# Two rings, a GpSimd-queue state load and a reordered first slot in the opening of an attention and MoE kernel

## The chip, the cores and the metric

The kernel runs on one core of one Trainium2 chip. The metric is device time of one execution in microseconds (us). "Median" is over all timed executions of a kernel in the state called fast; the profile is of one execution, and its span is some 2 us shorter than the time of that execution (205.1 us against 206.87 us for the kernel before). Engines are written as the profile has them: PE is TensorE, PEld its weight loads, DVE VectorE, ACT ScalarE, POOL GpSimd, SP SyncE.

## The reference, cut to what matters

```python
B, H, S, Ns, D = 8, 8, 512, 32, 64
def attn(x, state):                       # x [B,H,S,D], state [B,H,Ns,D]
    a = softmax(x @ state^T / 8)          # over the 32 state rows
    xread = a @ state
    a2 = softmax(state @ x^T / 8)         # over the 512 rows of x
    sread = a2 @ x
    return concat(xread, sread)           # [B,H,544,D] -> 4352 tokens of 512
def moe(x, w_in, w_out):                  # w_in [512,2048], w_out [2048,512]
    return gelu(x @ w_in) @ w_out
```

The kernel works batch by batch. The first Gelu of batch 0 can only start when x and state of batch 0 have been loaded, transposed, multiplied, exponentiated and normalised, and when a part of `w_in` is there. All that is "the opening", the first 12 of some 205 us.

## The kernel before

Cuts are marked with `# ...`. The inputs, all fp32, go either through a hardware ring (issued by SyncE or ScalarE; a cast follows on an engine) or through GpSimd's queue, whose target is a bf16 tile, with no cast behind it (in the list of DMA issues the state of batch 0 is 64.0 KB on ScalarE's ring, that of batch 1 32.0 KB on GpSimd's queue). All weights, and x of batches 1 to 7, are issued on GpSimd's queue, in program order.

```python
# opening, loads of batch 0: state and one quarter of x on ScalarE's ring, three quarters on SyncE's
nc.scalar.dma_start(out=st_f, in_=st_rows[:, 0, :, :])
for q in range(4):
    eng = nc.scalar if q == 2 else nc.sync
    eng.dma_start(out=x0f[:, q, :, :], in_=x0_rows[:, q, :, :])
# ...
nc.gpsimd.memset(sbd, 0.0)          # block-diagonal state, all eight batches
# ...
load_w_in(0, 256)                   # GpSimd's queue: the weight stream
load_w_in(256, 512)
load_w_out(0)                       # a quarter of w_out, 0.5 MiB in bf16
load_w_in(512, 1024)
load_st(1, 2)

def load_rest():                    # the stream after x of batch 1
    load_w_out(1); load_w_in(1024, 1536); load_w_out(2)
    load_w_in(1536, 2048); load_st(2, 3); load_x(2)
    load_w_out(3); load_x(3)

def keep_warm(n):                   # fillers: n x 128 columns of matmul on zeros
    ...

def state0():
    nc.scalar.copy(out=st_bf[:, 0, :, :], in_=st_f)    # cast
    # 5 transposes on TensorE, copies out of PSUM on VectorE
def cast0(q): ...                   # fp32 -> bf16 of one quarter of x
def xtr0(q): ...                    # its transposes and the copy out of PSUM
def scores0(q): ...                 # its scores and exp
def sums0(q): ...                   # its row sums
def norm0(t): ...                   # t = 0 multiplies on GpSimd, t = 1 on VectorE

keep_warm(31)
cast0(0); st0 = state0(); xtr0(0); cast0(1); state0_p(st0)
keep_warm(3)
cast0(2); xtr0(1); scores0(0); xtr0(2); cast0(3)
keep_warm(2)
scores0(1); sums0(0); xtr0(3); scores0(2)
keep_warm(2)
sums0(1)
load_x(1)                           # issue on GpSimd, ahead of the multiplication
norm0(0); scores0(3); sums0(2); sums0(3); norm0(1)
load_rest()
# ... P of batch 0 (attention folded with w_in) in two halves round the Gelu table load
# ... two matmul pairs "hp" and their Gelus, then the first slot
```

TensorE takes these instructions in program order.

The softmax here doesn't subtract the row's maximum and nothing guards it: scores larger than these inputs give would overflow.

## Time and profile before

| | before |
|---|---|
| time, median of 3 (later 4) runs | 206.78 us (206.87) |
| profiled span | 205.1 us |
| batch 0's state: landed, transposes start | 4.02, 4.61 us |
| first Gelu of batch 0 | 12.40 us |
| x of batch 2 landed | 31.53 us |
| scores of batch 2 start | 40.98 us |
| wait of TensorE for transposed x of batch 2 | 0.9 us |

From about 45 us on TensorE never stops (each stretch of 5 us up to 200 us reads 5.00 busy), so the end of the kernel is the moment at which the dense part starts plus a fixed amount of work. What sets that moment is the later of two arrivals near 41 us: TensorE itself, with the work of batches 0 and 1 behind it, and the transposed x of batch 2, which hangs on GpSimd's queue. In the trace of the kernel before, the x arrived last, by 0.9 us. The prediction shows the lines.

### The profile page before, as it was taken

How to read it: one execution, taken by the hardware profiler on the slowest of the kernel's cores; microseconds unless marked ns; L12 is line 12 of the kernel's file. 1: busy time of each engine (PE TensorE's matmuls, PEld its weight loads, DVE VectorE, ACT ScalarE, POOL GpSimd, SP SyncE). 2: the span in 40 equal slices, each digit the busy share in tenths (PEclk: the TensorE clock that was granted, in tenths of full speed). 3: DMA queues.
4: the chain of work that ended last, by engine and by line, in shares of the span. 5: the costliest groups of instructions: out<-in, count | busy, mean ns of one | idle time of the engine just before them, and what ended most of it. 6: DMA issues, size and time to landing. Idle time of an engine off the chain costs nothing.

```text
span 205.1 us, 4749 instructions
## 1 busy us (share of the span) xinstructions
PE 198.5 (97%) x1982; PEld 133.7 (65%) x1988; DVE 142.7 (70%) x227; ACT 134.3 (65%) x242; POOL 69.5 (34%) x74
## 2 busy tenths in 40 slices
PE   7899999899999999999999999999999999999994
PEld 2545444346776567766776777667775788778893
DVE  2944786989499868976697757765778553165883
ACT  3864786689696679675967697587857476744120
POOL 8964303632319645371626602330320001200000
PEclk9999999999999999999999999999999999999999
DMA  6999999689095687846574408450108001030125
GB/s 199 194 174 205 206 199 203 142 150 190 6 132 115 208 107 92 168 148 60 64 158 139 105 0 114 119 133 0 53 14 194 3 0 51 3 153 0 54 96 161
DMA packets 40533, 23.14 MB, mean 113 GB/s; under 512 B 21824, under 2 KB 39104, under 8 KB 40512
## 3 DMA queue, kind: packets, MB, share of 16 engines
q0 software_dynamic: 13952, 8.10, 28.8%
q1 hardware_dynamic: 25872, 14.36, 28.8%
q10 hardware_dynamic: 688, 0.39, 0.6%
q8 instruction: 15, 0.25, 0.5%
q14 instruction: 6, 0.05, 0.1%
HBM read 17.30 MB, written 8.91 MB: 128 GB/s over the span
## 4 chain that ended last, share of the span: by engine, by line
PE 79%; DMA 15%; POOL 5%; issue 0%; DVE 0%; POOLq 0%
PE xp L573 40%; PE hp L464 23%; DMA xb<-in_x_dram 11%; PE p_ps L420 4%; DMA xT<-x 4%; PE hps L505 3%; PE rp L749 3%; POOL w_in_bf L105 2%; PE xp L679 2%; PE pt L329 1%; PE sr L383 1%; POOL x L223 1%; PE op L490 1%; POOL sbd L95 1%; POOL w_out_bf L113 0%
## 5 line engine op out<-in xcount | busy, mean ns | idle before, releaser
L471 ACT ACTIVATE g<-hp 128x512 bf16<-128x512 f32 x124 | 67.3, 602 | 28.2 <-PE hp L464 21.2
L464 PE MATMUL hp<-AT,P 128*128 128x512 bf16 x248 | 63.4, 379 | 0.1
L573 PEld LDWEIGHTS <-gsum 128*128 128x128 bf16 x528 | 51.2, 98 | 13.1 <-issue 2.1
L567 DVE TENSOR_TENSOR gsum<-g 128x2048 bf16<-128x2048 bf16 x35 | 45.9, 1328 | 0.1
L573 PE MATMUL xp<-ws,gsum 128*128 128x256 bf16 x304 | 36.3, 273 | 0.0
L464 PEld LDWEIGHTS <-P 128*128 128x128 bf16 x248 | 22.9, 98 | 19.7 <-issue 2.3
L573 PE MATMUL xp<-ws,g 128*128 128x256 bf16 x224 | 26.8, 273 | 0.0
L573 PE MATMUL xp<-w_out_bf,gsum 128*128 128x256 bf16 x224 | 26.6, 273 | 0.0
L432 DVE CAST P<-p_ps 128x512 bf16<-128x512 f32 x30 | 19.6, 686 | 9.4 <-PE p_ps L420 9.3
L573 PEld LDWEIGHTS <-g 128*128 128x128 bf16 x224 | 21.8, 98 | 5.1 <-issue 0.2
L622 POOL TENSOR_TENSOR u<-s,oh 128x512 f32<-128x512 f32 x6 | 9.1, 1518 | 40.7 <-ACT oh L619 40.7
L431 ACT CAST P<-p_ps 128x512 bf16<-128x512 f32 x30 | 16.7, 598 | 5.4 <-PE p_ps L420 5.0
L223 POOL COPY x<-xb 128x1024 bf16<-128x1024 bf16 x12 | 13.6, 1162 | 16.6 <-DMA xb<-in_x_dram 11.5
L233 POOL COPY xo<-xb 128x1024 bf16<-128x1024 bf16 x12 | 14.7, 1252 | 4.4 <-PE sr L383 4.4
L592 POOL TENSOR_TENSOR v<-q,oh 128x512 f32<-128x512 f32 x6 | 9.0, 1494 | 20.4 <-ACT oh L624 17.2
L616 DVE TENSOR_TENSOR s<-xp,s 128x512 f32<-128x512 f32 x6 | 4.2, 692 | 11.3 <-PE xp L573 11.3
L420 PE MATMUL p_ps<-w_in_bf,sbd 64*32 64x512 bf16 x248 | 11.4, 383 | 0.1
L352 DVE TENSOR_TENSOR a<-e,ics 128x512 bf16<-128x512 bf16 x14 | 10.7, 763 | 0.6 <-DVE ics L351 0.2
L595 DVE TENSOR_TENSOR oh<-xp,v 128x512 f32<-128x512 f32 x6 | 4.2, 692 | 9.8 <-POOL v L592 9.8
L336 ACT ACT_TABLE_LOAD x7 | 9.0, 1283 | 0.9 <-PE pt L329 0.8
L628 DVE TENSOR_TENSOR q<-xp,s 128x512 f32<-128x512 f32 x6 | 4.1, 685 | 7.8 <-PE xp L573 7.8
L349 DVE TENSOR_REDUCE cs<-e 128x16 f32<-128x512 bf16 x14 | 9.5, 677 | 0.0
(111 smaller groups left out, 220.1 us busy)
## 6 DMA issues: line engine op xcount, KB each, us to landing
out_dram<-oh SPq DMA_DIRECT2D x15, 256.0 KB, 2.4
xb<-in_x_dram POOLq DMA_DIRECT2D x7, 512.0 KB, 6.1
out_dram<-oh SPq DMA_DIRECT2D x6, 512.0 KB, 2.8
w_out_bf<-in_moe_w_out_dram POOLq DMA_DIRECT2D x4, 512.0 KB, 11.8
w_in_bf<-in_moe_w_in_dram POOLq DMA_DIRECT2D x6, 256.0 KB, 11.6
out_dram<-osb SPq DMA_DIRECT2D x5, 256.0 KB, 3.1
x0f<-in_x_dram SPq DMA_DIRECT2D x3, 256.0 KB, 3.7
w_in_bf<-in_moe_w_in_dram POOLq DMA_DIRECT2D x4, 128.0 KB, 3.7
```

Of the source, the lines that this page charges most:

```text
L223: nc.gpsimd.tensor_copy(out=A.x4[:, :, :, 64 * t:64 * t + 64].rearrange("p j c d -> p c j d"), in_=src[:, t],)
L233: eng.tensor_copy(out=A.xo[:, :, :, 2 + 64 * t:66 + 64 * t].rearrange("p j c d -> p c j d"), in_=src[:, t],)
L349: nc.vector.reduce_sum(out=cs, in_=e4, axis=AX.X)
L352: nc.vector.tensor_tensor(out=A.a[:, :, hs].rearrange("p g (c n) -> p g c n", n=NS), in0=e4, in1=ics[:, :, :].to_broadcast((128, G, 2, NS) ...
L420: nc.tensor.matmul(ps[t][32 * c:32 * c + 32, :], lhsT=sbd[64 * t:64 * t + 64, b, c, 32 * t:32 * t + 32], rhs=w_in_bf[64 * t:64 * t + 64, c ...
L431: nc.scalar.copy(out=dst[:, 0, :], in_=ps[0])
L432: nc.vector.tensor_copy(out=dst[:, 1, :], in_=ps[1])
L464: nc.tensor.matmul(hp, lhsT=Ps[b][:, t, m * 128:(m + 1) * 128], rhs=atts[b].AT[:, :, t, :], start=(t == 0), stop=(t == 1),)
L471: nc.scalar.activation(out=gs[b][:, m, :], in_=hp, func=AF.Gelu)
L567: nc.vector.tensor_tensor(out=t, in0=g_q(b, h0, k0), in1=g_q(b, h1, k1), op=op)
L573: nc.tensor.matmul(ps[:, j - js[0], :], lhsT=lhs[:, m, 128 * j:128 * j + 128], rhs=rhs[:, m, :], start=(first and j == js[0] and m == 0), ...
L622: nc.gpsimd.tensor_tensor(out=xs[b, "u"], in0=xs[b, "s34"], in1=o, op=ALU.subtract)
```

## The change

Its intent: load x of batch 0 over two rings at once, take the state's load and cast off ScalarE, let the normalisation's multiplication run ahead of an issue that had held it up, hand out `w_out` in half chunks so that TensorE's first slot does not wait for it, and reorder that slot. The diff, cut to its core:

```diff
-    nc.scalar.dma_start(out=st_f, in_=st_rows[:, 0, :, :])
     for q in range(4):
-        eng = nc.scalar if q == 2 else nc.sync
-        eng.dma_start(out=x0f[:, q, :, :], in_=x0_rows[:, q, :, :])
+        eng = nc.scalar if q % 2 else nc.sync
+        for u in ((slice(0, 1), slice(1, 2)) if q == 2 else (slice(0, 2),)):
+            eng.dma_start(out=x0f[:, q, u, :], in_=x0_rows[:, q, u, :])
...
-    nc.gpsimd.memset(sbd, 0.0)
+    nc.vector.memset(sbd[:, 0:B // 2], 0.0)
...
-    load_w_in(0, 256)
-    load_w_in(256, 512)
-    load_w_out(0)
+    load_st(0, 1)
+    nc.gpsimd.memset(sbd[:, B // 2:B], 0.0)
+    load_w_in(0, 512)
+    load_w_out(0, 2)
+    load_w_out(2, 4)
...                                    (load_rest: w_out in halves, same order)
     def state0():
-        nc.scalar.copy(out=st_bf[:, 0, :, :], in_=st_f)
...                                    (PSUM copies: state to ScalarE, x to VectorE;
                                        ScalarE casts quarter 3 instead of 1)
-    keep_warm(31)
+    keep_warm(28)
     cast0(0)
+    cast0(1)
     st0 = state0()
     xtr0(0)
+    xtr0(1)
+    cast0(3)
+    scores0(0)
+    cast0(2)
+    scores0(1)
+    keep_warm(2)
+    xtr0(2)
...
     norm0(1)
+    load_x(1)                         (was ahead of norm0(0))
     load_rest()
...                                    (P of batch 0 in one piece; fillers 2+12+3 -> 8)
+    turn[0] = 3
...
-    M(6)
+    M(6, 7)
+    sread(0)
+    sread_out(0)
     begin(1)
     xtr(1, (0, 1))
     xtr(1, (2, 3))
-    sread(0)
-    sread_out(0)
-    M(7)
     scores(1, 0)
+    mm2_m(0, 4)
     scores(1, 1)
     srt(0)
-    U(4, 5)
+    mm2_m(0, 5)
...
```

More of the change, by code (lines that the diff above doesn't have):

```diff
@@ L71 @@
     g_sr = persist.tile([128, MC, B * NS], BF16, name="g_sr")
-    st_f = persist.tile([128, 2, D], FP32, name="st_f")
     st_bf = persist.tile([128, B, 2, D], BF16, name="st_bf")
@@ L110, with load_w_out @@
     w_out_r = moe_w_out.rearrange("(m p) n -> p m n", p=128)
-    def load_w_out(i):
-        nc.gpsimd.dma_start(out=w_out_bf[:, 4 * i:4 * i + 4, :], in_=w_out_r[:, 4 * i:4 * i + 4, :])
+    def load_w_out(m0, m1):
+        nc.gpsimd.dma_start(out=w_out_bf[:, m0:m1, :], in_=w_out_r[:, m0:m1, :])
     def load_x(b):
@@ L133, in load_rest @@
     def load_rest():
-        load_w_out(1)
+        load_w_out(4, 6)
+        load_w_out(6, 8)
         load_w_in(1024, 1536)
-        load_w_out(2)
+        load_w_out(8, 10)
+        load_w_out(10, 12)
         load_w_in(1536, 2048)
@@ L139, in load_rest @@
         load_x(2)
-        load_w_out(3)
+        load_w_out(12, 16)
         load_x(3)
@@ L189, in state0 @@
             h = slice(64 * u, 64 * u + 64)
-            nc.vector.tensor_copy(out=sb0[h, :, :, u, :], in_=ps[h, 0:2, u:HC:2, :])
+            nc.scalar.copy(out=sb0[h, :, :, u, :], in_=ps[h, 0:2, u:HC:2, :])
         return ps
@@ L239, in cast0 @@
     def cast0(q):
-        copy = nc.scalar.copy if q == 1 else nc.vector.tensor_copy
+        copy = nc.scalar.copy if q == 3 else nc.vector.tensor_copy
         copy(
@@ L257, in xtr0 @@
             )
-        copy = nc.scalar.copy if q == 2 else nc.vector.tensor_copy
-        copy(out=xT0[:, q, :, :], in_=ps)
+        nc.vector.tensor_copy(out=xT0[:, q, :, :], in_=ps)
     def xtr(b, cs):
@@ L435, in pmat, with pmat00 @@
         p_copy(b, f, p_mm(b, f, ftile))
-    def pmat00(h):
-        if h == 0:
-            Ps[0] = att.tile([128, 2, d_ff], BF16, name="P", tag="P")
-        ps = [otile([128, 256], "p_ps") for t in range(2)]
-        for c in range(HC):
-            for t in range(2):
-                nc.tensor.matmul(
-                    ps[t][32 * c:32 * c + 32, :],
-                    lhsT=sbd[64 * t:64 * t + 64, 0, c, 32 * t:32 * t + 32],
-                    rhs=w_in_bf[64 * t:64 * t + 64, c, 256 * h:256 * h + 256],
-                    start=True,
-                    stop=True,
-                )
-        for t in range(2):
-            nc.scalar.copy(out=Ps[0][:, t, 256 * h:256 * h + 256], in_=ps[t])
+    def pmat00():
+        Ps[0] = att.tile([128, 2, d_ff], BF16, name="P", tag="P")
+        ps = p_mm(0, 0, otile)
+        for h in range(2):
+            for t in range(2):
+                n = slice(256 * h, 256 * h + 256)
+                nc.scalar.copy(out=Ps[0][:, t, n], in_=ps[t][:, n])
     gs = {}
@@ L809 @@
     begin_e(0)
-    keep_warm(31)
+    keep_warm(28)
     cast0(0)
+    cast0(1)
     st0 = state0()
     xtr0(0)
-    cast0(1)
-    state0_p(st0)
-    keep_warm(3)
-    cast0(2)
-    xtr0(1)
-    scores0(0)
-    xtr0(2)
-    cast0(3)
-    keep_warm(2)
-    scores0(1)
-    sums0(0)
-    xtr0(3)
+    xtr0(1)
[5 more added lines that the diff above has]
+    xtr0(2)
+    sums0(0)
+    sums0(1)
+    xtr0(3)
+    norm0(0)
+    state0_p(st0)
     scores0(2)
-    keep_warm(2)
-    sums0(1)
-    load_x(1)
-    norm0(0)
     scores0(3)
@@ L834 @@
     norm0(1)
+    load_x(1)
     load_rest()
-    keep_warm(2)
-    pmat00(0)
     nc.scalar.activation(out=gate, in_=gate, func=AF.Gelu)
-    keep_warm(12)
+    keep_warm(8)
     atr(0, (0,))
-    keep_warm(3)
-    pmat00(1)
+    pmat00()
     atr(0, (1,))
@@ L872 @@
     xtr(1, (2, 3))
-    sread(0)
-    sread_out(0)
-    M(7)
     scores(1, 0)
+    mm2_m(0, 4)
     scores(1, 1)
     srt(0)
-    U(4, 5)
+    mm2_m(0, 5)
     rearr_ones(1)
     w_sums(2)
-    U(6)
+    mm2_m(0, 6)
     pmat(0, 2)
@@ L885 @@
     norm(1, 1)
-    U(7)
+    mm2_m(0, 7)
     M(8, 9)
```

## The prediction

> **What bounds the kernel now.** I read the page first, for the share of each engine:
>
> ```profile
> span 205.1 us, 4749 instructions
> PE 198.5 (97%) x1982; PEld 133.7 (65%) x1988; DVE 142.7 (70%) x227; ACT 134.3 (65%) x242; POOL 69.5 (34%) x74
> PEclk9999999999999999999999999999999999999999
> ```
>
> TensorE is busy 97% of the span and never loses its clock. So the kernel is TensorE's work plus whatever holes there are, and only 205.1 - 198.5 = 6.6 us of holes exist. Next, the busy time in stretches of 5 us, to see where they lie (columns: stretch and its length, then busy us and instructions of PE, weight load, VectorE, ScalarE, GpSimd, then clock, DMA share, GB/s):
>
> ```profile
> 5.00:10.00 5.00, 4.52 (x49) 2.85 (x48) 4.39 (x14) 4.17 (x11) 5.00 (x8) 1.00 1.31 197
> 20.00:25.00 5.00, 4.67 (x49) 2.21 (x42) 3.85 (x8) 3.26 (x5) 1.68 (x2) 1.00 1.24 206
> 40.00:45.00 5.00, 4.01 (x45) 1.78 (x46) 4.30 (x6) 4.16 (x6) 2.70 (x3) 1.00 0.62 112
> 45.00:50.00 5.00, 5.00 (x42) 2.99 (x42) 4.86 (x9) 4.99 (x11) 0.06 (x1) 1.00 1.03 181
> ```
>
> Every stretch from 45 us up to 200 us reads 5.00: there TensorE is dense, and the change touches nothing there. So a gain exists only if it brings forward the moment, near 41 us, at which that dense part starts. Third, TensorE's own waits over the whole run:
>
> ```profile
> PE warm_ps L148 <- DVE warm L92: 1.2, 1, 1.2
> PE pt L329 <- DMA xT<-x: 0.9, 1, 0.9
> PE aT_ps L366 <- POOL a L314: 0.5, 1, 0.5
> PE op L490 <- DMA w_out_bf<-in_moe_w_out_dram: 0.3, 1, 0.3
> ```
>
> The last hole before the dense part is the second line: the scores of batch 2 wait for the transposed x of batch 2. Fourth, the chain of waits that ended last, for what that transposed x hangs on:
>
> ```profile
> 8.24 10.20 DMA xb<-in_x_dram
> 18.44 0.28 issue
> 18.72 12.81 DMA xb<-in_x_dram
> 31.53 0.05 issue
> 31.59 2.03 POOL x L223 x2
> 33.61 0.02 issue
> 33.63 7.30 DMA xT<-x
> 40.93 0.05 issue
> 40.98 0.64 PE pt L329 x16
> ```
>
> x of batch 2 lands at 31.53, GpSimd rearranges it for 2.03 us, the DMA transpose takes 7.30 us, and at 40.98 TensorE starts. No TensorE work is in this chain before 40.98. That is the central reading: up to 41 us the end is set by GpSimd's DMA queue, and TensorE, whose last matmuls before it were issued by about 39.9 (the last group starts at 39.02, four matmuls at 0.216 us apart), already waits about 1.1 us for it.
>
> That queue is limited by bandwidth, not by when its DMAs are issued. Between the landings at 18.44 and 31.53 it delivers w_out 0.5, w_in 0.5, w_out 0.5, w_in 0.5, state 0.03 and x 0.5 MiB: 2.53 MiB = 2.65 MB in 13.09 us, 203 GB/s written, and the stretches from 14 to 34 us read 190 to 207 GB/s. As the source is fp32 and the destination bf16, the read side moves twice that.
>
> [...] while batch 0's x is read (2.5 to 5 us) the engines already move 308 to 381 GB/s, with one load on a second ring; then the weight stream takes over at 190 to 205. So two rings can reorder landings but hardly shorten their sum. [...] the multiplication of the second half of the normalisation took 1.11 us on VectorE beside GpSimd's one, while the same shape in later batches (another line) takes 0.69 us alone. [...]
>
> **The change part by part.** These lines of the timeline (start us, us, engine, line, operation) carry the end of the opening:
>
> ```profile
> 9.17 1.12 POOL L314 TENSOR_TENSOR a<-e,ics 128x512 bf16<-128x512 bf16 x1
> 9.62 1.28 ACT L838 ACT_TABLE_LOAD   x1
> 9.74 1.11 DVE L314 TENSOR_TENSOR a<-e,ics 128x512 bf16<-128x512 bf16 x1
> 11.20 0.65 ACT L454 CAST P<-p_ps 128x256 bf16<-128x256 f32 x2
> 12.40 2.06 ACT L862 ACTIVATE g<-hp 128x512 bf16<-128x512 f32 x4 [0.55 <-PE hp L854]
> ```
>
> *x and state of batch 0.* Now the four quarters land near 3.8, 4.9, 5.4 and 6.3 us (issue time plus 3.0 to 4.6 us to landing). With two rings from the start, quarters 0 and 1 share the engines: I estimate 4.2 for both (0.4 later, 0.7 earlier) and the last still about 6.0. The state leaves ScalarE's ring: its 64 KB (0.17 us at 370 GB/s) and its 0.30 us cast go, a GpSimd issue of 0.76 us comes, landing at an estimated 4.3 instead of 4.04. The transposes of the state began at 4.61 behind the 8 filler matmuls (8 x 0.427 from 1.19 = 4.60); 28 fillers end at 4.18. Net: state ready about when it was.
>
> *VectorE.* Between the first cast at 3.81 and the reciprocal that ends at 8.81 it has seven other pieces of 0.41 to 0.49 us and two 0.22 us copies, with one idle stretch of 1.06. After: the two copies go to ScalarE, one cast and one PSUM copy change engines, the pieces run 4.2 to about 8.9 at a pitch of 0.35 to 0.42, with one wait for quarter 2. The same time, +0.1.
>
> *Normalisation.* GpSimd's multiplication starts at 9.17, though its reciprocal was ready at 8.81, because the issue of batch 1's x held GpSimd from 8.24 to 9.21. Ahead of the issue it gains up to 0.36 us; with the reciprocal 0.1 later, 0.2 to 0.3.
>
> *P of batch 0.* Before, two of its four PSUM copies (0.65) ran ahead of the Gelu table load, two after. Now all four, 4 x 0.33 = 1.3 us, come after table load and gate. Exp of the last quarter I put at 9.1 to 9.5, as its PSUM copy now stands behind two sums on VectorE; the load ends at 10.8, the gate at 11.0, the copies at 12.3. The first Gelu then starts at about 12.4 to 12.6, against 12.40. So the opening ends where it did: -0.2 to +0.4 us.
>
> *First slot.* Batch 0's read-out (0.36 us of TensorE) and another matmul pair (0.43) go ahead of the transposes of batch 1's x, and w_out arrives in half chunks, with matmuls ordered to use each as it lands. Before, 12 matmuls from 21.06 should take 12 x 0.216 = 2.6 us and the next group began at 24.23: 0.5 us lost to w_out. This hole should close: -0.5 us for TensorE's arrival, which is then near 39.4 +- 0.4 instead of 39.9.
>
> *The queue that sets the end.* Same order, same 4.56 MiB up to batch 2's x. Differences: 64 KB fewer on the hardware rings (-0.17), 32 KB more here in small pieces (+0.1), the first w_in half in 2 KB rows instead of 1 KB, whose stretch read 184 to 198 GB/s against 200 to 207 later (0.5 MiB at 203 instead of 193: -0.13). GpSimd's sequence gets 0.9 us (half the clear of the block-diagonal state) plus 2 x 0.63 (two w_in issues) shorter and 0.76 + 3 x 0.78 longer, but 1 to 2 MiB are queued at any time, so no byte waits for it. Batch 2's x shifts by about -0.2, and the rearrangement and the transpose (2.03 + 7.30) follow it unchanged, as the transpose still shares the engines with the same last w_out chunk and x of batch 3.
>
> Sum: the end moves by the queue's -0.2 us, not by TensorE's -0.5; the wait before the scores of batch 2 grows from 0.9 to about 1.2. From 206.78 that is 206.6; I take 206.4, as there are dips in the queue (153 to 166 GB/s at 8 to 9 us, 117 to 168 at 11 to 13, together some 0.8 us against 200) of which another order may remove some.
>
> **The rivals.** (1) The opening's gain arrives at the end. It needs the transposed x of batch 2 to come earlier too. For it: the chain of waits begins with GpSimd's clear and issues, which the change shortens. Against: the queue holds a backlog of at least 1 MiB, and x of batch 2 lands 12.8 us after its issue, 0.5 MiB of which would take 2.6 us. If it held, 205.3 to 205.7. (2) The queue runs dry. Batch 1's x is now issued behind the normalisation, at about 10 instead of 8.24, when some 0.5 MiB is still queued, and the 8 DMAs that seem allowed in flight (issue 13 waited for number 5's landing, issue 17 for number 9's) now hold fewer bytes. [...] +0.3 to +0.8 us, 207.1 to 207.6. (3) Fewer fillers (38 units of 128 columns against 55) let the clock drop in the opening: 1 to 3 us of TensorE time, of which 1.1 to 1.5 are hidden by the same wait; 207 to 209. The clock row without a dip and the real transposes in between speak against it. (4) ScalarE becomes the bound of the opening, by over 1 us, through a cast that waits for the last x ahead of the first exp: up to 1 us hidden, so 206.8 to 207.3.
>
> **Range and chances.** The first outcome (queue sets the end) has some 60%, rival 1 20%, the slower ones 20%. With run-to-run spread of about +-0.5 (206.3 to 207.32 before), 8 in 10 lie between 205.3 and 207.5. Two per cent is 4.1 us: all holes before 41 us together, fillers aside, are less, so faster by over 2% gets 0.03; slower, which needs a clock drop and a starved queue together, 0.02; within, 0.95.
>
> **What would show each step.** Right: TensorE's wait for the transposed x of batch 2 still there and not shorter than 0.9 us; x of batch 2 landing at 31.3 +- 0.5; its transpose again near 7 us; the w_out wait gone; the first Gelu at 12.2 to 12.8; GpSimd's multiplication no longer behind the issue; four P copies in a row after the table load; clock row unchanged; every stretch after 45 us full. Wrong: that wait gone, or the landing of x of batch 2 a whole microsecond off either way; then the queue is not bound by bandwidth as I read it, and the end follows the opening or the order of issues.

## The result, and the profile after

| | before | after |
|---|---|---|
| time, median (lowest to highest), 4 runs each | 206.87 us (206.3 to 207.32) | 209.23 us (208.74 to 210.01) |
| ratio, 95% interval | | 1.0119 (1.0079 to 1.016) |
| transposes of the state start | 4.61 us | 6.55 us |
| first Gelu of batch 0 | 12.40 us | 15.63 us |
| x of batch 2 rearranged from | 31.59 us | 33.78 us |
| scores of batch 2 start | 40.98 us | 43.23 us |

Ratios here and below are the mean time of one kernel's runs over that of the other's of the same rounds, so they are not quite the ratios of the medians. Executions over 1.5% slower than the fastest of the same kernel are left out of the means. The change costs 1.2%, some 2.4 us: within 2%, but clearly slower, and outside the predicted range of 205.3 to 207.5. The profiled run of the kernel after is its slowest (210.01), so durations in its trace are a little on the long side.

The page of the kernel after, its head, its busy times and its row of TensorE's clock:

```profile
span 208.2 us, 4726 instructions
PE 199.8 (96%) x1969; PEld 133.9 (64%) x1974; DVE 142.1 (68%) x227; ACT 133.9 (64%) x242; POOL 67.9 (33%) x76
PEclk9999999999999999999999999999999999999999
```

The span is 3.1 us longer, with 1.3 us more of busy TensorE for 13 fewer matmuls: some matmuls ran longer. The clock row shows nothing of it, and cannot. The list of clock changes kept with the trace begins, for this run, at 15.61 us, with full clock; the row counts the time before its first entry as full. (In the kernel before, the first entry is at 6.89 us.) The stretches, in the columns of the prediction's table:

```profile
5.00:10.00 5.00, 3.33 (x30) 2.46 (x30) 1.58 (x6) 2.31 (x7) 2.85 (x5) 1.00 1.17 164
40.00:45.00 5.00, 4.95 (x44) 2.34 (x43) 4.41 (x6) 3.54 (x6) 1.81 (x3) 1.00 0.74 93
45.00:50.00 5.00, 4.99 (x44) 2.77 (x37) 4.86 (x10) 4.96 (x9) 0.33 (x1) 1.00 1.16 218
```

From 5 to 10 us TensorE is busy 3.33 us instead of 4.52, with 30 instructions instead of 49. From 40 to 45 us, where the wait for x of batch 2 used to be, it is nearly full: that hole is gone, but not because anything came early. TensorE's largest wait over the whole run:

```profile
PE st_ps L180 <- DMA st_bf<-in_state_dram: 2.2, 1, 2.2
```

One new wait of 2.2 us, for the DMA of batch 0's state. And the chain that ended last now begins with that same DMA and then runs through the opening and TensorE, not through GpSimd's queue:

```profile
1.44 5.07 DMA st_bf<-in_state_dram
...
11.37 1.06 POOL a L315
...
14.18 2.56 PE hp L842 x8
```

The timeline of the kernel after (start us, us, engine, line, operation, and what ended the idle time before it) has the mechanism:

```profile
1.44 0.86 POOL L120 DMA_DIRECT2D st_bf<-in_state_dram  x1
...
6.55 0.43 PE L180 MATMUL st_ps<-ident,st_bf 128*64 128x128 bf16 x4 [2.19 <-DMA st_bf<-in_state_dram]
...
11.37 1.05 POOL L315 TENSOR_TENSOR a<-e,ics 128x512 bf16<-128x512 bf16 x1 [3.52 <-DVE ics L313]
...
12.36 0.96 POOL L116 DMA_DIRECT2D xb<-in_x_dram  x1
...
14.53 0.15 PEld L842 LDWEIGHTS <-P 128*128 128x128 bf16 x1 [0.28 <-ACT P L447]
14.96 0.15 PEld L842 LDWEIGHTS <-P 128*128 128x128 bf16 x1 [0.28 <-issue]
15.63 2.07 ACT L850 ACTIVATE g<-hp 128x512 bf16<-128x512 f32 x4 [0.73 <-PE hp L842]
```

Three things are to be seen. First, the state's DMA starts to be issued at 1.44 us and lands at 6.51, though it is 32 KB; the quarters of x land at 4.24, 4.58, 5.70 and (the halved one) 4.95 and 6.27. The smallest load lands last of all, and TensorE, whose program has the state's transposes first, idles 2.19 us with two quarters of x already cast. Second, near 15 us the weight loads of consecutive 512-column matmuls are 0.43 us apart, where such matmuls elsewhere in the run take 0.216: TensorE runs at half its rate, 8 us after the wait has ended. At 15.61, where the list of clock changes begins with full clock, the distance falls to 0.216. (The 8 fillers that the prediction counts took 0.427 each, the same rate, called cold here; the first fillers do so in all 20 traces.) In this run the clock had not come up before the wait and so did not fall: it stayed at half until 15.61. Third, GpSimd idles 3.52 us ahead of its multiplication and issues x of batch 1 only at 12.36 instead of 8.24.

Windows of 2 us place it. The kernel before, from 4 us, where the wait will be, and from 14 us:

```profile
4.00:6.00 2.00, 2.00 (x14) 1.05 (x13) 0.90 (x4) 1.05 (x3) 2.00 (x4) 1.00 1.21 310
...
14.00:16.00 2.00, 2.00 (x18) 0.75 (x16) 0.00 (x0) 0.46 (x1) 0.98 (x3) 1.00 1.51 190
```

And the kernel after, the same windows:

```profile
4.00:6.00 2.00, 0.36 (x1) 0.00 (x0) 0.77 (x2) 0.00 (x0) 2.00 (x4) 1.00 1.30 281
...
14.00:16.00 2.00, 2.00 (x8) 0.75 (x7) 1.45 (x5) 1.27 (x5) 2.00 (x5) 1.00 1.16 115
```

In the second row of each TensorE is "busy" the full 2.00 us, but with 18 matmuls before and 8 after. That count overstates it: 8 of the 18 are small ones that start side by side at 15.96, and 2 of the 8 are transposes, so of full-size ones there are 10 against 6. Equal busy time, less work: that is how a cold clock looks where the clock column (1.00 in both) does not show it. The distance of equal matmuls, 0.43 against 0.216 us, is the surer sign. The last column says the other thing: the DMA engines moved 115 GB/s instead of 190 there. The last load issued ahead of x of batch 1 landed at 15.46 (15.76 before), x of batch 1 itself only at 20.52 (18.44 before): the queue was not late up to there, and ran dry while x of batch 1 was held back.

How much of the 3.2 us at the first Gelu reaches the end? Before, TensorE's arrival had a slack of about 1.1 us at the transposed x of batch 2; 3.2 - 1.1 = 2.1, near the 2.25 us by which the scores of batch 2 start later and the 2.4 us of the medians. From the first Gelu to those scores it is 28.6 us before, of which about 1 is waiting, and 27.6 us after: apart from the wait, the first slot took as long as it did before. In the profiled run another 0.8 us was lost later (162.0 us from these scores to the last matmul instead of 161.2; TensorE is 4.79 us busy of the 5 from 70 us, 5.00 before), which fits its being the slowest of the four runs. The clock's story, too, is that of one run: the record gives the other three a mean clock of 0.981, 0.992 and 0.992, which I estimate as 7.9, 3.3 and 3.3 us at half clock ((1 - 0.992) x 2 x 207.4; the lists of clock changes of the two kernels' traces hold no other value than 1.0 and 0.5). In those the clock seems to have been up and to have fallen for a while, where in the profiled run it came up late.

### The profile page after: what moved, and what is told of

It is laid out like the page before. It is cut to its first block, busy times and chain, and to the rows that moved or that the text cites.

```text
span 208.2 us, 4726 instructions
## 1 busy us (share of the span) xinstructions
PE 199.8 (96%) x1969; PEld 133.9 (64%) x1974; DVE 142.1 (68%) x227; ACT 133.9 (64%) x242; POOL 67.9 (33%) x76
## 4 chain that ended last, share of the span: by engine, by line
PE 81%; DVE 10%; POOL 3%; DMA 2%; issue 1%; POOLq 0%; DVEq 0%
PE xp L566 35%; PE hp L457 23%; PE p_ps L421 4%; PE op L511 3%; PE hps L498 3%; PE rp L742 3%; DVE gsum L560 2%; DMA st_bf<-in_state_dram 2%; PE op L483 2%; PE xp L672 2%; PE pt L330 1%; POOL x L225 1%; PE hp L842 1%; DVE P L433 1%; DVE ws L532 1%; DVE a L353 1%
## 5 line engine op out<-in xcount | busy, mean ns | idle before, releaser
L615 POOL TENSOR_TENSOR u<-s,oh 128x512 f32<-128x512 f32 x6 | 8.0, 1328 | 40.7 <-ACT oh L612 40.7
L225 POOL COPY x<-xb 128x1024 bf16<-128x1024 bf16 x12 | 13.1, 1126 | 14.6 <-DMA xb<-in_x_dram 8.4
L421 PE MATMUL p_ps<-w_in_bf,sbd 64*32 64x512 bf16 x256 | 12.3, 390 | 0.3 <-DVE srm L398 0.3
L609 DVE TENSOR_TENSOR s<-xp,s 128x512 f32<-128x512 f32 x6 | 4.1, 692 | 11.3 <-PE xp L566 11.3
L511 PE MATMUL op<-w_out_bf,g 128*128 128x512 bf16 x44 | 11.5, 380 | 0.2
L411 DVE COPY XSR<-srT 128x128 bf16<-128x128 bf16 x8 | 5.7, 759 | 5.7 <-PE srT L408 5.7
```

The lines of the kernel that those rows point to most:

```text
L225: nc.gpsimd.tensor_copy(out=A.x4[:, :, :, 64 * t:64 * t + 64].rearrange("p j c d -> p c j d"), in_=src[:, t],)
L421: nc.tensor.matmul(ps[t][32 * c:32 * c + 32, :], lhsT=sbd[64 * t:64 * t + 64, b, c, 32 * t:32 * t + 32], rhs=w_in_bf[64 * t:64 * t + 64, c ...
L511: nc.tensor.matmul(ops[b, j], lhsT=gs[b][:, m, j * 128:(j + 1) * 128], rhs=w_out_bf[:, m, :], start=(m == 0), stop=(m == MC - 1),)
```

## The experiments

My theory after reading the traces: the state, moved from a hardware ring to GpSimd's queue, has to share the DMA engines with x on two rings and lands 2 us late (6.51 us against an estimated 4.3); the wait also keeps TensorE's clock low (matmuls 0.43 us apart up to 15.61 us); both together delay the first Gelu by 3 us. The rival: the state only happens to be the last wait, and the two rings, the late issue of batch 1's x (a queue run dry) or the thinned fillers cost the time. In the diffs only the lines of the edit are shown; "before" in brackets is the median of the kernel before in the same call. All kernels gave a correct result.

### First call: the state, the fillers and the order

**a_state_ring**: the kernel after with the state back on ScalarE's ring.

```diff
+    nc.scalar.dma_start(out=st_f, in_=st_rows[:, 0, :, :])     # ahead of x
-    load_st(0, 1)
     def state0():
+        nc.scalar.copy(out=st_bf[:, 0, :, :], in_=st_f)
```

> The kernel after, with the state of batch 0 alone put back: fp32 on ScalarE's ring ahead of x, cast on ScalarE; everything else of the change kept. Theory S (the state in GpSimd's queue lands behind all of x and holds TensorE, in order, for 2.2 us; a cold clock follows from that wait): state usable near 4.4 us, first Gelu back from 15.6 to 12.3-12.9, TensorE's wait for the transposed x of batch 2 back at 0.7 to 1.5 us, time 206.2 to 207.0. Rival R (the loss is in the rest: normalisation ahead of the issue, P copies all behind the table load, fewer fillers): first Gelu still after 14, time 208.5 or more.

Measured: 208.76 us (206.7), ratio 1.0103 (1.0043 to 1.0164). The wait for the state went, and yet the time hardly moved (1.0103 against 1.0119, far inside either interval). In its timeline, ScalarE's cast of x's last quarter:

```profile
8.59 0.62 ACT L245 CAST x0b<-x0f 128x512 bf16<-128x512 f32 x1 [3.22 <-DMA x0f<-in_x_dram]
```

That quarter landed at 8.5 us, 6.8 us after its issue, and ScalarE, whose program has its cast ahead of the first exp, ran that exp only at 9.23 (at 6.25 in **t_exp_first**, which has them the other way round). The clock reads 0.50 from 8 to 14 us here, and the first Gelu started at 15.03. So undoing the guilty part alone uncovers a second way of being late. My explanation lies in the neighbour: without a state issue at the head of GpSimd's queue the weight stream starts at 2.14 us, 0.86 earlier than in the kernel before (3.0), and takes the DMA engines while x is still moving. That is a theory at this point; **v_ring_full_clear** tests it.

**b_state_queue**: the kernel before with nothing changed but the state's load, to the head of GpSimd's queue.

```diff
-    nc.scalar.dma_start(out=st_f, in_=st_rows[:, 0, :, :])
-    nc.gpsimd.memset(sbd, 0.0)
+    load_st(0, 1)
+    nc.gpsimd.memset(sbd, 0.0)
     load_w_in(0, 256)
     def state0():
-        nc.scalar.copy(out=st_bf[:, 0, :, :], in_=st_f)
```

> The kernel before, with the state of batch 0 alone moved to the head of GpSimd's queue as bf16. Theory S: it lands at 6.0 to 6.6 us as in the kernel after, TensorE waits about 2 us for it, first Gelu at 14.5 to 15.5 instead of 12.4, of which about 1.1 is hidden by the wait for the transposed x of batch 2: time 208.0 to 209.2. Rival R: the state lands under 5 us or its lateness is hidden, time within 0.6 of the kernel before.

Measured: 208.12 us (206.7), ratio 1.0078 (1.0015 to 1.0141). Among TensorE's waits:

```profile
PE st_ps L176 <- DMA st_bf<-in_state_dram: 1.8, 1, 1.8
PE pt L327 <- DMA xT<-x: 0.4, 1, 0.4
```

The transposes started at 6.35 and the first Gelu at 14.06 (12.40 before). Moving one 32 KB load costs 0.8% (0.15 to 1.4%) by itself, some two thirds of the change's 1.2%. This is the central result for the theory, and x lies mostly on one ring here, so the second ring is not needed for the lateness: the state landed 4.9 us after its issue. But not all of the 0.8% is TensorE's wait for the state. The second line above says that the scores of batch 2 (42.25 us) still waited 0.4 us for x of batch 2, which was rearranged from 33.56 instead of 31.59. The edit puts the state's issue ahead of the clear, and the weight stream starts at 4.04 instead of 3.00. TensorE alone would have been ready at about 41.8, 0.8 us later than before; the rest came through the queue.

**c_fillers**: the kernel after with fillers up to the state's landing.

```diff
-    keep_warm(28)
+    keep_warm(48)
```

> The kernel after with 48 filler units instead of 28 ahead of the state's transposes, so that TensorE stays busy until about 6.3 us, just before the state lands at 6.5. If the idle 2.2 us left the clock cold until 15.7 us, the matmuls of the first Gelus go from 0.43 to 0.22 us apart, and the time falls by 0.7 to 1.2 us to 208.0 to 208.6. If the lateness alone costs the time, it stays within 0.3 of 209.2, and matmuls stay 0.43 apart or the gain is hidden.

Measured: 207.84 us (206.7), ratio 1.0057 (1.001 to 1.0103). The state is as late as ever, only the hole is filled with matmuls on zeros. The first Gelu came at 13.82 instead of 15.63 and its four took the same 2.06 us:

```profile
13.82 2.06 ACT L850 ACTIVATE g<-hp 128x512 bf16<-128x512 f32 x4 [0.20 <-PE hp L842]
```

The large matmuls ahead of it were 0.215 us apart (one 0.33) instead of 0.43. So about half of the loss (1.0119 to 1.0057, 0.6% or 1.3 us) seems to be not the wait but the cold clock that goes with it in the trace of the kernel after. As the two ratios come from different calls, each uncertain by 0.4 to 0.5%, the size is an estimate. The runs of c support it from another side: two had a mean clock of 1.000 and took 207.36 and 207.37 us, two had 0.992 and took 208.30 and 208.75. So even these fillers seem not to have kept the clock up in every run, and losing it to have cost some 1.2 us.

**d_x_first**: the kernel after with the transposes of x ahead of those of the state, so that TensorE has work as soon as x is cast.

```diff
-    st0 = state0()
     xtr0(0)
     xtr0(1)
+    st0 = state0()
```

> The kernel after with the transposes of the first two quarters of x put ahead of those of the state in TensorE's order. x landed at 4.2 and 4.5, so these and their PSUM copies can run in the wait; what is left behind the state's landing is shorter by 0.5 to 0.9 us, and TensorE idles less before it. Theory S: time 208.0 to 208.8, first Gelu 14.6 to 15.1. If the time does not fall, another engine than TensorE (VectorE or ScalarE's order) carries the delay after the state has landed.

Measured: 208.97 us (206.7), ratio 1.0108 (1.007 to 1.0146). I expected a gain and was wrong. The wait for the state shrank to 0.7 us, but with 8 short transposes in the hole (1.03 us of the 2.1) the clock did not come up in the profiled run: the eight large matmuls took 3.39 us, and the first Gelu came at 14.97. That a hole has to be filled densely, as in c, is suggested by this and not shown: see "What they say together" for how much chance there is in the clock of one run.

### Second call: the other parts one by one, on the kernel before

**e_slot_only**: first slot reordered, `w_out` in halves, nothing else.

```diff
+    turn[0] = 3
-    load_w_out(0)
+    load_w_out(0, 2)
+    load_w_out(2, 4)                      # and so on, as in the change
-    M(6)
+    M(6, 7); sread(0); sread_out(0)       # and so on, as in the change
```

> The kernel before with only the first slot reordered and w_out in half chunks. If the end is set near 41 us by the transposed x of batch 2, closing the 0.5 us hole at the second w_out chunk is hidden: that hole gone, the wait for the transposed x grown to about 1.3 us, time within 0.3 of the kernel before. If instead TensorE sets it, 0.4 to 0.6 us faster.

Measured: 206.77 us (207.24), ratio 0.9991 (0.996 to 1.0022). The time is as expected, but the reason is not. The half chunk is one more issue on GpSimd ahead of the normalisation, whose multiplication starts at 9.85 instead of 9.17; the first Gelu comes at 13.09 instead of 12.40. The scores of batch 2 do not wait at all:

```profile
40.81 0.63 PE L332 MATMUL pt<-sbd,xT 128*128 128x64 bf16 x16
```

The transposed x was there at 39.48. So this run does not show that a faster TensorE would gain nothing, as in its trace TensorE arrived last, only 0.17 us earlier than the scores of batch 2 started before. And the reordered slot is not seen to be faster: from the first Gelu to these scores it takes 27.7 us here, and 27.6 us before without the 0.9 us of waiting, though the wait for `w_out` is gone.

**g_slot_x2**: the same, with x of batch 2 issued ahead of the half chunk of `w_out` before it.

```diff
-        load_w_out(10, 12)
         load_w_in(1536, 2048)
         load_st(2, 3)
         load_x(2)
+        load_w_out(10, 12)
```

> The same, and x of batch 2 loaded ahead of the third w_out chunk's second half (0.25 MiB, 1.25 us at 203 GB/s). If the transposed x of batch 2 sets the end: it comes about 1.2 us earlier, TensorE's wait for it falls to about 0, and the time falls by 0.8 to 1.5 us below the kernel before (205.2 to 205.9). If it does not set the end, or the load of batch 3's x slows the transpose as before until it is done, under 0.4 us.

Measured: 206.69 us (207.24), ratio 0.998 (0.9952 to 1.0007): a tendency, not shown. x of batch 2 landed at 30.74 (32.22 in e) and there is no wait for it, as in e; but in the profiled run one quarter of batch 0's x landed late (its cast at 7.35), so the first Gelu was at 13.82 and the gain of the queue met a later TensorE. Nothing in the edit, which comes after the opening, explains that late landing; I leave it open.

**h_rings_only**: x of batch 0 over two rings as in the change; the state stays on ScalarE's ring ahead of it.

```diff
-        eng = nc.scalar if q == 2 else nc.sync
-        eng.dma_start(out=x0f[:, q, :, :], in_=x0_rows[:, q, :, :])
+        eng = nc.scalar if q % 2 else nc.sync
+        for u in ((slice(0, 1), slice(1, 2)) if q == 2 else (slice(0, 2),)):
+            eng.dma_start(out=x0f[:, q, u, :], in_=x0_rows[:, q, u, :])
```

> The kernel before with only x of batch 0 spread over the two rings as in the kernel after (quarters 1 and 3 behind the state on ScalarE's ring, the third in two halves). Theory Q (a last piece of the opening, shared out with the weight stream, lands late): quarter 1, cast on ScalarE, lands later than 5.0 and quarter 3 near or after 6.3 us; first Gelu 12.4 to 13.2; time +0.0 to +0.8, partly hidden by the wait for x of batch 2. If two rings help, first Gelu under 12.2 and the time unchanged or lower.

Measured: 207.75 us (207.24), ratio 1.0028 (0.9997 to 1.006). The first Gelu was at 12.40, exactly where it was: the second ring gains nothing in the opening. But the rearrangement of x of batch 2 began at 33.34 instead of 31.59, and TensorE's wait for it grew from 0.9:

```profile
PE pt L330 <- DMA xT<-x: 1.7, 1, 1.7
```

GpSimd issued its loads at the same times as in the kernel before (the first weights at 3.00, x of batch 1 at 8.24), but x of batch 1 took 11.0 us to land instead of 10.2, and the queue moved 171 GB/s instead of 190 from 14 to 16 us. Why two rings early should slow the queue later I cannot say from these traces. It may not be the rings: in run k, below, whose DMAs are those of the kernel before, x of batch 1 took 11.3 us to land.

**i_norm_only**: the issue of batch 1's x moved behind the normalisation.

```diff
     sums0(1)
-    load_x(1)
     norm0(0)
     # ...
     norm0(1)
+    load_x(1)
     load_rest()
```

> The kernel before with only the order on GpSimd changed: the normalisation ahead of the issue of batch 1's x, which moves behind the second normalisation. As predicted: the multiplication starts 0.2 to 0.36 us earlier than 9.17, first Gelu 12.1 to 12.4, x of batch 2 lands as before (31.2 to 31.9), time within 0.3. If the queue runs dry, the rate dips near 11 to 13 us, x of batch 2 lands after 32, time +0.4 to +0.9.

Measured: 207.6 us (207.24), ratio 1.002 (0.9989 to 1.005). The multiplication started at 8.97 instead of 9.17 and the first Gelu at 12.12 instead of 12.40, as predicted. x of batch 1 was issued at 9.97 instead of 8.24 and the rearrangement of x of batch 2 began at 33.33; the scores of batch 2 started at 42.02. So the opening's gain is real, and in this trace a later queue eats it: TensorE waits 0.7 us for x of batch 2. How much of the slip is the edit's doing is open, as the DMA engines moved 151 GB/s from 6 to 8 us (190 before), ahead of anything that the edit touches.

### Third call: how long the state takes alone, and what a warm clock is worth

**l_state_alone**: the kernel after, with both rings held by a small copy that reads the state, so that x starts only when the state has landed. Slow on purpose.

```diff
+    for i, eng in enumerate((nc.sync, nc.scalar)):
+        eng.dma_start(out=scr[:, i, :], in_=st_bf[:, 0, i, :])   # waits for the state
     for q in range(4):
         # x over two rings, as in the change
```

> The kernel after, with both hardware rings held until the state has landed (a small copy out of the state goes ahead of x on each). Only the landing of the state is read; the kernel is slower on purpose. If the state landed at 6.5 because it shared the engines with x of batch 0, it lands at 3.6 to 4.5 us here. If the path or its 128-byte pieces are slow by themselves, it lands after 5.5.

Measured: 216.53 us, one look. In the list of DMA issues (engine, operation, count, KB, us from issue to landing) of this run, the state of batch 0:

```profile
st_bf<-in_state_dram POOLq DMA_DIRECT2D x1, 32.0 KB, 2.5
```

And in the kernel after:

```profile
st_bf<-in_state_dram POOLq DMA_DIRECT2D x1, 32.0 KB, 5.1
```

The same issue at the head of the same queue lands in 2.5 us with x held back and in 5.1 us beside 1 MiB of x on the rings. The lateness comes from having x beside it, not from GpSimd's way of issuing as such. Alone it landed at 3.90 us, before the 4.3 that the prediction had put down. What l cannot part is the sharing of the engines from the place in line: in the kernel after, four of the five loads of x are issued ahead of the state (0.74 to 1.25 us against 1.44), and an issue of the state ahead of x on GpSimd was not tried.

**j_ring_fillers**: a_state_ring with the holes filled (28 to 31 at the start, 2 to 12 ahead of the third quarter's transposes, and 28 more ahead of the fourth's).

```diff
-    keep_warm(28)
+    keep_warm(31)
-    keep_warm(2)
+    keep_warm(12)
     xtr0(2)
     # ...
+    keep_warm(28)
     xtr0(3)
```

> The kernel after with the state back on ScalarE's ring, as in the first experiment, plus fillers in TensorE's gaps of the opening (31 units at the start, 12 instead of 2 before the third quarter's transposes, 28 more before the fourth's). If the cold clock (granted 0.50 from 8 to 14 us in that run) costs most of what was left, the first Gelu comes at 13.2 to 14.2 and the time falls from 208.8 to 207.2-207.9. If the last quarter's landing ahead of ScalarE's first exp is what costs, under 0.4 us is gained.

Measured: 208.1 us (207.26), ratio 1.0086 (1.0031 to 1.0141). In the profiled run the clock stayed up, the first Gelu came at 13.67 against 15.03 of a_state_ring, and 1.3 us of opening were still missing: x's last quarter, landed 5.6 us after its issue, was cast at 7.44. The scores of batch 2 start at 41.21 in this run (207.72 us), only 0.2 us later than before; the mean is raised by a run of 210.28 us, of which there is no trace.

**p_slot_states**: e_slot_only, with the small states of batches 1 and 2 taken out of GpSimd's queue. They go in fp32 over SyncE's ring behind x and VectorE casts them in its free time.

```diff
+    nc.sync.dma_start(out=st_f[:, 1:3, :, :], in_=st_rows[:, 1:3, :, :])
-    load_st(1, 2)
-        load_st(2, 3)
     for q in range(4):
         ones0(q)
+    nc.vector.tensor_copy(out=st_bf[:, 1:3, :, :], in_=st_f[:, 1:3, :, :])
```

> The kernel before with the reordered first slot, and the states of batches 1 and 2 loaded as fp32 on the sync ring behind x and cast on VectorE, instead of as 128-byte pieces in GpSimd's queue. If each such small load holds the queue for some 0.7 us (the rate falls to 75 to 140 GB/s around them), x of batch 2 lands 1 to 2 us earlier than in the same slot order without it (32.3), and the time is 0.4 to 1.0 below the kernel before. If the dips have another cause, no change: within 0.3.

Measured: 206.33 us (207.26), ratio 0.9976 (0.9946 to 1.0007); one of its six runs (209.77) is left out. The queue's first dip, which the prediction had seen but not explained, looks like the small state load. The window in the kernel before:

```profile
8.00:10.00 2.00, 1.64 (x20) 0.65 (x18) 1.90 (x7) 1.85 (x6) 2.00 (x3) 1.00 1.20 176
```

The same window in this run:

```profile
8.00:10.00 2.00, 1.58 (x18) 0.60 (x16) 1.90 (x7) 1.75 (x5) 2.00 (x3) 1.00 1.32 203
```

203 GB/s instead of 176, and 205 instead of 168 in the next 2 us; e, which differs in the small states alone, has 180 and 168. x of batch 2 landed at 31.03 and the scores of batch 2 started at 39.93, without a wait. Most of the earlier start is not the landing, though: the transpose of this x took 5.1 us instead of 7.3.

**m_before_again**: the kernel before, unchanged, for the spread of the landing times.

```diff
 (no edit)
```

> The kernel before once more, unchanged, for the spread of its own trace. If the landing of batch 2's x is steady, it is within 0.5 us of 31.6 as in the first trace, and the 33.3 us seen with the rings alone and with the normalisation alone are their doing. If it moves by itself, it lies anywhere from 31.5 to 33.5 and those two say little.

Measured: 206.12 us, one look. x of batch 2 landed so that its rearrangement began at 31.58 (31.59 in the first profile), the first Gelu was at 12.41 (12.40), the wait 0.8 (0.9). Two traces alike speak against spread as the cause of the 33.3 us of h and i, but they are few: in k, with the same DMAs, the rearrangement began at 32.18.

### Fourth call: fillers, the change without its start, and the best version

**k_fewer_fillers**: the kernel before with its fillers cut to 38 units from 55, as the change has them (the expectation says 40; the edit leaves 28, 2 and 8).

```diff
-    keep_warm(31)
+    keep_warm(28)
-    keep_warm(3)                # and two of the three of two
-    keep_warm(12)
+    keep_warm(8)
-    keep_warm(3)
```

> The kernel before with only its fillers cut to those of the kernel after (28 at the start, 2, 2 and 8 later, 40 units instead of 55). If the clock is lost through TensorE's wait for late data and not through the smaller number of fillers, the clock warms up before 7 us as it did and the time stays within 0.3. If fewer fillers are enough to keep it cold, the matmuls of the first Gelus are 0.43 us apart and the time is 0.8 to 1.5 above the kernel before.

Measured: 206.65 us (206.66), ratio 0.9983 (0.9945 to 1.0021). In the profiled run the clock stayed up: the eight large matmuls took 2.02 us. Two of the four runs have a mean clock of 0.992, so it was not up in all of them, yet they took 206.61 and 206.81 us. Fewer fillers alone cost nothing that these runs show. The trace has one more thing: the scores of batch 2 start at 40.44 without waiting for x of batch 2, whose transpose took 5.1 us and was done at 39.32. So in the kernel before the two arrivals are so close that either can be the last.

**s_after_old_start**: the change without its start: state on the ring, x mostly on one ring, casts and copies on their old engines; kept are the normalisation ahead of the issue, P in one piece, the split clear and the weight pieces, and the slot. The fillers are the old ones too.

```diff
 (the kernel before, plus:)
+    nc.vector.memset(sbd[:, 0:B // 2], 0.0)
+    nc.gpsimd.memset(sbd[:, B // 2:B], 0.0)
+    load_w_in(0, 512)
     # norm0, load_x(1), pmat00, first slot, w_out halves: as in the change
```

> The kernel after without the three parts found guilty so far: state on ScalarE's ring and x mostly on the sync ring as before, the old order of casts and the old fillers; kept are the normalisation ahead of the issue, all four P copies behind the table load, w_in and w_out in the new pieces, the split clear and the reordered slot. If those three explain the loss, first Gelu 12.0 to 12.7 and time within 0.5 of the kernel before. If something kept costs too (P copies, queue), 207.4 or more.

Measured: 206.96 us (206.66), ratio 1.000 (0.9948 to 1.0053). Without its start the change costs nothing. Here too the last quarter of x was late (6.4 us to its landing; the weight stream starts early in this kernel as well) and the first Gelu was at 13.63, yet the time equals that of before. The trace says where it goes: the scores of batch 2 start at 41.16, only 0.18 us later than before, as the 1.2 us are for the most part hidden where the kernel before waited 0.9 us for x of batch 2. The interval (plus or minus 0.5%, 1.1 us) hides the rest.

**r_states_norm**: p_slot_states plus the normalisation ahead of the issue.

```diff
 (p_slot_states, plus:)
-    load_x(1)                   # ahead of norm0(0)
     norm0(0)
     # ...
     norm0(1)
+    load_x(1)
```

> The last faster kernel (reordered slot, states of batches 1 and 2 as fp32 on the sync ring) with the normalisation ahead of the issue as well. With x of batch 2 landing early enough not to be waited for, the 0.28 us that this order gave the first Gelu should now reach the end: 0.2 to 0.4 below the run of the same call without it. If the queue runs dry from the later issue, it is the same or slower.

Measured: 206.06 us (206.66), ratio 0.9962 (0.9931 to 0.9994). The best version found, and the only one whose interval lies below 1: 0.4% faster than the kernel before, so faster than both. First Gelu at 12.15, wait for x of batch 2 0.5 us. The profile is of its slowest run (206.66; the others took 206.04 to 206.27), and x of batch 2 landed at 31.77 there, no earlier than before: what makes it faster is not shown.

**p_again**: p_slot_states once more, beside it.

```diff
 (p_slot_states, unchanged)
```

> The reordered slot with the states of batches 1 and 2 on the sync ring, unchanged, once more, as the first interval (0.9946 to 1.0007) just touched 1 with one run of six at 209.8. Expected 0.3 to 0.9 us below the kernel before, x of batch 2 landing at 31.1, no wait for its transpose.

Measured: 206.39 us (206.66), ratio 0.9974 (0.9943 to 1.0004). The first p result (0.9976) repeats. The early landing does not: x of batch 2 landed at 31.53 here, as in the kernel before, but its transpose took 5.3 us and the scores started at 39.89. Between p and r the intervals overlap; that r is better than p is not shown.

### Last two: which of the two late things in a and j

**t_exp_first**: j_ring_fillers with ScalarE's cast of the last quarter behind the second exp, so that ScalarE never holds an exp behind a landing.

```diff
-    cast0(3)
     scores0(0)
     cast0(2)
     scores0(1)
+    cast0(3)
```

> The run with the state on the ring and fillers in the gaps (208.1, first Gelu 13.7), with one thing moved: the cast of the last quarter of x, on ScalarE, stands behind the exps of the first two quarters instead of ahead of both. If ScalarE's order made the rest of the loss, the first exp comes at 6.2 to 6.8 instead of 8.1, the first Gelu 0.4 to 1.0 earlier, and the time falls to 207.0-207.7. If the late landing of that quarter itself bounds the opening, exps early but first Gelu within 0.3 of 13.7 and the time within 0.4 of 208.1.

Measured: 208.42 us (206.94), ratio 1.0067 (1.0024 to 1.0109). In its timeline the first exp and the first Gelu:

```profile
6.25 0.38 ACT L300 ACTIVATE e<-pc 128x256 bf16<-128x256 f32 x1 [0.80 <-PE pc L293]
...
13.66 0.60 ACT L853 ACTIVATE g<-hp 128x512 bf16<-128x512 f32 x1 [0.19 <-PE hp L845]
```

The first exp runs 3 us earlier than in a_state_ring (9.23), and the first Gelu stands where it stood in j (13.67). So the order on ScalarE was not the cost. What is left is x's last quarter (cast at 8.51 here, at its landing) or the 28 fillers ahead of its transposes, which end near 9.1 as well; this run cannot part the two.

**v_ring_full_clear**: a_state_ring with GpSimd clearing the whole block-diagonal state again, which puts the first weight issue back to 3.00 us.

```diff
-    nc.vector.memset(sbd[:, 0:B // 2], 0.0)
-    nc.gpsimd.memset(sbd[:, B // 2:B], 0.0)
+    nc.gpsimd.memset(sbd, 0.0)
```

> The first experiment (state back on ScalarE's ring, 208.8) with one thing more: GpSimd clears the whole block-diagonal state again, as in the kernel before, so that the weight stream's first issue moves from 2.14 to 3.0 us. In all four runs with that issue at 2.14 the last quarter of x took 5.6 to 6.8 us to land, in all but one with it at 3.0 or later 4.3 to 4.9. If the earlier weight stream pushes x back: last landing under 5.0 us after its issue (by 6.3 to 6.7), first Gelu 12.2 to 13.2 instead of 15.0, time 206.3 to 207.3. If not: landing 5.6 or more again and time above 208.

Measured: 208.29 us (207.28), ratio 1.0041 (1.0003 to 1.0079); one run of the kernel before took 339.39 us and is left out. x's last quarter landed 4.4 us after its issue (6.8 in a) and its cast ran at 6.19 instead of 8.59; the multiplication of the normalisation started at 8.93. So the start of the weight stream delays x: of the runs looked at for it, those whose first weight issue came at 3.0 us or later had the last of x 4.3 to 4.9 us after its issue, and those at 2.14 us (a, j, t, and s with x on the old rings) 5.6 to 6.8 us. (The exception is g, with 6.1 us at the old start.) v is also the cleanest undoing of the state's move, as the stream starts at 3.00 in it and at 3.19 in the kernel after: 1.0041 against 1.0119, the same 0.8% as in b. The windows of v show one thing that still costs:

```profile
8.00:10.00 2.00, 0.72 (x6) 0.23 (x6) 1.60 (x6) 1.37 (x3) 1.07 (x2) 1.00 1.12 171
...
12.00:14.00 2.00, 2.00 (x6) 0.73 (x5) 1.25 (x5) 1.27 (x4) 1.35 (x3) 0.50 1.24 204
```

TensorE is busy only 0.72 us of the 2 from 8 us, in pieces with no single gap over 0.9 us, and from about 11 to 14.5 us it runs at half clock: 6 matmuls fill 2 us, and here the column says so (0.50). First Gelu at 13.07; the scores of batch 2 start at 41.39, 0.4 us later than before. (The profiled run, the slowest of the four, lost another 1.3 us after them.) The cut fillers may be the reason for the half clock, but no run has both v's edit and more fillers; that stays open.

### What they say together

| part | alone, against before |
|---|---|
| state to GpSimd's queue (b) | +0.78% (shown) |
| x over two rings (h) | +0.28% (not quite shown) |
| normalisation ahead of the issue (i) | +0.20% (not shown) |
| slot and half chunks (e) | -0.09% (none shown) |
| all of it (after) | +1.19% |

The sum of the four is 1.17%, close to the whole, but that closeness is worth little: each is uncertain by 0.3 to 0.6%, and taking the state's part out again (a) wins back only 0.16%, not 0.78%, until the stream's start is put back too (v). The parts interact, through two things that no part owns: who has the DMA engines in the first 6 us (x's last quarter lands 4.3 to 6.8 us after its issue), and whether TensorE has its clock (the large matmuls ahead of the first Gelus are 0.43 us apart in the trace of the kernel after, 0.215 in that of c).

The clock has its share of chance. In the 18 traces that hold clock changes (those of c and e hold none), the changes within a trace lie multiples of 3.41 us apart (7.66 and 11.07 us in b; 6.89 and 204.86, 58 times 3.413, in the kernel before), and where the first falls differs from run to run: 4.68 us in m, 6.89 in the first trace of the same kernel. In b the clock was 0.50 between those two moments, after TensorE's wait of 1.8 us for the state. How busy TensorE was between two of these moments goes some way to tell what the clock did next (it came up only after stretches 82 to 100% busy; it fell after 40% in b, 42% in g, 61% and 60% in a and v), but not all the way: in s it stayed up after 49%. So the clock of a single profile is one draw, and what c, d and k say of it is to be read so.

## Why the prediction was right or wrong

**Right in the traces it read, but too firm: what bounds the kernel before.** The end is set by GpSimd's queue through x of batch 2 in both traces of that kernel (waits of 0.9 and 0.8 us), and i fits it (an earlier first Gelu, a later queue, no gain). But e and k, with nearly the same opening, do not wait for x of batch 2 at all, and x landed no earlier in p_again and r than before. The queue and TensorE arrive within about 1 us of each other, and the length of the transpose (7.3 us before, 5.1 to 5.2 in e, k and p) is enough to change which is last. In the kernel after it was TensorE: the transposed x was there at 41.78, the scores started at 43.23.

**Right: most small items.** The `w_out` wait is gone; the P copies stand four in a row behind the table load (13.70 us, 1.20 us in all); the multiplication no longer stands behind the issue. Alone (i) it gained 0.2 us, as worked out. The "-0.5 us for TensorE's arrival" from the first slot is not seen: from the first Gelu to the scores of batch 2 it took 27.6 us after, 27.6 before without the wait. Nor did the transpose follow unchanged: 5.95 us instead of 7.30.

**Wrong, and the step that decides: "x and state of batch 0".** The prediction put the state's landing "at an estimated 4.3 instead of 4.04" and concluded "Net: state ready about when it was". It landed at 6.51. The estimate holds for a state with no x beside it: issue at 1.44 plus the 2.5 us of run l is 3.9. Beside x on two rings the same load took 5.1 us. The prediction had let x share the engines with x ("quarters 0 and 1 share the engines"), but not the small load with x. Its times for x itself were good: 4.2 for the first two quarters and 6.0 for the last, against 4.24, 4.58 and 6.27 (6.3 for the last before, so two rings did not shorten the sum).

**Wrong in consequence: "-0.2 to +0.4 us" for the opening.** It was +3.2 us at the first Gelu. The fillers of run c won back 1.8 of them in its profiled run, which is the cold clock's part; the other 1.4 stay with the late state and the new order behind it. Of the end, c puts the clock's part at about 1.3 us, an estimate.

**Wrong: the dismissal of rival (3).** The prediction had the right effect, at a size for which it shows no figure, "1 to 3 us of TensorE time, of which 1.1 to 1.5 are hidden by the same wait; 207 to 209", and set it aside because of "the clock row without a dip and the real transposes in between". The clock row of before says nothing of a kernel with another hole in it, and it reads 9 even where the prediction's own fillers take 0.427 us, at half clock; the row of the kernel after has no dip either, though its matmuls run at half rate; and in run d the transposes in the hole did not bring the clock up (eight large matmuls in 3.39 us, 2.02 in k). The trigger was not the one named: fewer fillers alone cost nothing (k); the late state made the hole (2.19 us).

**Wrong in size: "the queue that sets the end".** "Batch 2's x shifts by about -0.2", and its landing was to be 31.3 +- 0.5. Its rearrangement began at 33.78 against 31.59. "No byte waits for it" failed: behind the normalisation, the issue of batch 1's x is tied to the opening, so a late opening starves the queue (115 GB/s from 14 to 16 us). That is rival (2), and it came with a larger cause than was named. It cost nothing in the kernel after, because TensorE came later still; the wait for x of batch 2 was gone, which the prediction listed as a sign of being wrong. In the traces of h and i, where the opening is on time, a rearrangement at 33.3 us is what the scores of batch 2 wait for.

**Open.** What the last 0.7 to 0.9% of j and t are, the late quarter, the fillers ahead of it or runs without a trace; how much of b's cost is the weight stream's later start; what makes r faster; how far x of batch 2 lands differently by itself from run to run; by which mechanism an earlier weight stream delays the rings' loads so much (that it does is shown by a against v).

## What to carry to other kernels

Before moving a small load to another queue, ask what else is on the DMA engines at that moment: its time alone (2.5 us here) says little about its time beside a megabyte on other rings (5.1 us here), and an engine whose program has it first waits for it, however small (TensorE 2.19 us for 32 KB, with two quarters of x already cast). Look for a cold TensorE in the distance of equal matmuls (0.43 against 0.216 us here) rather than in the clock row (9 throughout), and do not take the clock of one profiled run for that of the kernel. When a time comes out as expected, look in the trace whether the reason did too (run e). And test a part by doing it alone as well as by undoing it alone: here doing it alone cost 0.78%, undoing it won 0.16%, and only both show that two parts hold each other.
